# Value products in blocks of four key tiles, and half of half the score tiles copied to SBUF by VectorE

## The chip, the cores and the metric

The kernel runs on one core of one Trainium2 chip. The metric is the device time of one execution in microseconds (us), lower is better. One percent here is 13.8 us.

## The reference

One layer of 2048 rows by 512 columns computes two branches from the same input and blends them row by row with a gate. All tensors are float32.

```python
g = sigmoid((x * gate_w).sum(-1, keepdims=True))
q = (x @ wq).reshape(B, S, H, Dh)      # S 2048, H 32 heads, Dh 16
k, v = x @ wk, x @ wv                  # one key and one value head for all 32
p = softmax(q @ k.T * Dh ** -0.5)      # 32 x 2048 x 2048
a = (p @ v).reshape(B, S, H * Dh) @ wo
b = (silu(x @ w_gate) * (x @ w_up)) @ w_down   # inner width 1792
out = g * a + (1 - g) * b
```

## The kernel before

**The work of the long middle part.** Attention is walked in 512 units: unit `u` is head `u // 16` and key tile `u % 16` of 128 keys. `score(u, j)` makes one score tile: 128 keys by 1024 queries in two banks of PSUM (`pss`), by two TensorE matmuls that use the upper and the lower 64 rows of the array at the same time. ScalarE then takes the exponential of the whole tile from PSUM into the row tile `pt` in SBUF (L613). The pool of `pss` has two buffers, so the matmuls of a score tile wait until the exponential of the tile two before it has read its buffer. `mix(u)` multiplies the exponentials of unit `u` with the values: four matmuls of 32 array columns each, side by side, in full float32, accumulated over the 16 units of a head in `po` (L622). The value tile `vaug` carries columns of ones, so `po` also gets the sums of the softmax.

**The second branch as filler.** The products of the gated feed-forward branch are cut into jobs of 12 or 15 terms (`gate_up`, `down`, and earlier `query`). Each term is split into the upper and the lower 64 rows, and `halves.step` issues one lower half of one job beside one upper half of another: one such step is a *feed*. When a job's last matmul is out, VectorE gets its result from PSUM (`pf`): a copy into `hs` for a gate product (L246), a multiplication for an up product (L257), an addition into `acc` for a down product. The hyperbolic tangent of a gate product runs on ScalarE (L251), and VectorE then forms the SiLU (L252) and splits the product into `hh` and `hl` (L97, L98).

**The order.** It is written by hand under `manual_schedule`: every engine executes its own instructions in the order in which the code issues them. The loop runs over `n` in steps of two units. In each step stand four score tiles, eight feeds, then `mix(u)` and `mix(u + 1)`, which is where the tangents (`ACTS`) and one piece of a finished head's normalization (`LATER`: four reciprocals of 128x128, one product and the store to `o_d`) are issued. Row tiles `pt` have three buffers. The sums of the second branch for all 2048 rows stay in one tile `acc`.

**The tail.** After the loop come the last eight jobs, undivided, and then `finish`, the output projection of the four chunks of rows in the order of `ORDER`.

Of the kernel before, what the change touches and what calls it, by code (L numbers as in the profile page):

```python
# [18 lines left out]
P = 128  # L19
S = 2048  # L20
D = 512
H = 32
# [21 lines left out]
KEEP = 6  # L44
RATE = 8
FIRST = 6
STOP = 5
EARLY = 12
PTB = 3
WRB = 2  # L50


@with_exitstack
def tile_gated_mix(ctx, tc, x, wq, wk, wv, wo, w_gate, w_up, w_down, gate_w, out):
# [35 lines left out]
        return XC[c]  # L90

    wp = tc.alloc_tile_pool(name="wp", bufs=2)
    ACC = []


    def split(hi, lo, src, eng=nc.gpsimd, eng_hi=nc.vector):
# [16 lines left out]
    ACTS, LOADS = [], []  # L113

    def run(queue, n):
        for _ in range(min(n, len(queue))):
            queue.pop(0)()

    def load_split(view, name, bufs, pool=wp):
        shape = list(view.shape)  # L120
# [106 lines left out]

    def open_acc():
        qpool.release()
        accp = tc.alloc_tile_pool(name="accp", bufs=1, side="right")  # L230
        ACC.extend([accp.tile([P, NT, D], F32, name="acc"), accp])

    def gate_up(n, c):
        t = []

        def project(nm):
            def terms():
                r = []
                for k in range(KD):
                    r += three(W[nm, n], XC[c], (slice(None), k), (slice(None), k))  # L240
                return r
            return terms

        def gate(ps):
            g = wp.tile([P, CH], F32, name="hs", bufs=2)
            nc.vector.tensor_copy(g, ps)  # L246

            t.append(wp.tile([P, CH], F32, name="ht", bufs=2))

            def silu():  # L250
                nc.scalar.activation(t[0], g, AF.Tanh, scale=0.5)  # L251
                nc.vector.scalar_tensor_tensor(t[0], t[0], 1.0, g, op0=ALU.add, op1=ALU.mult)  # L252

            ACTS.append(silu)

        def up(ps):
            nc.vector.tensor_tensor(t[0], t[0], ps, ALU.mult)  # L257
            hh = wp.tile([P, CH], F32R, name="hh", bufs=7)
            hl = wp.tile([P, CH], F32R, name="hl", bufs=7)
            split(hh, hl, t[0], nc.vector)  # L260
            HT[n] = (hh, hl)

        r = []
        for nm, end in (("g", gate), ("u", up)):
            r.append(Job(3 * KD, lambda nm=nm: (nm, n) in W and c in XC, project(nm), end))
            r[-1].after.append(lambda nm=nm: load_w(nm, n + 2))
        return r

    def down(ns, c, i):
        t = c * TC + i  # L270

        def ready():
            return all(n in HT and ("d", n) in W for n in ns)

        def terms():
            r = []
            for n in ns:
                r += three(HT[n], W["d", n], (slice(None), slice(i * P, (i + 1) * P)), slice(None))
            return r

        def add(ps):
            acc = ACC[0]
            if ns[0] % NF == 0:
                nc.vector.tensor_scalar(acc[:, t, :], ps, c_sb[:, t:t + 1], None, op0=ALU.mult)
            else:
                nc.vector.scalar_tensor_tensor(acc[:, t, :], ps, c_sb[:, t:t + 1], acc[:, t, :],
                                               op0=ALU.mult, op1=ALU.add)

        return Job(3 * len(ns), ready, terms, add)

    def store_acc(c):
        nc.sync.dma_start(a_d[c], ACC[0][:, c * TC:(c + 1) * TC, :])


    def jobs():
# [23 lines left out]
    def whole(job):  # L319
        for i in range(job.size):  # L320
            job.step(i)
        run(ACTS, 1)


    def fill(n):
# [60 lines left out]
    def finish(c, pool):  # L386
        for i in range(TC):
            t = c * TC + i
            ps = ps_f.tile([P, CH], F32, name="pf")
            terms = []  # L390
            for k in range(KD):
                terms += three([x[:, k] for x in OT[c]], WO[k], (slice(None), slice(i * P, (i + 1) * P)), slice(None))
            mm(ps, terms)
            ot = pool.tile([P, D], F32, name="ot", bufs=4)
            parts = 2 if c == ORDER[-1] and i == TC - 1 else 1
            for j in range(parts):
                w = slice(j * D // parts, (j + 1) * D // parts)
                nc.vector.scalar_tensor_tensor(ot[:, w], ps[:, w], g_sb[:, t:t + 1], ACC[0][:, t, w], op0=ALU.mult, op1=ALU.add)  # L398
                (nc.scalar if j else nc.sync).dma_start(out[t * P:(t + 1) * P, w], ot[:, w])


# [189 lines left out]
    with tc.tile_pool(name="bpool", bufs=2) as bp:  # L591
# [8 lines left out]
                nc.sync.dma_start(qs[b * RT + DH:(b + 1) * RT], qv[b])  # L600


        def score(u, j):
            h, kt = divmod(u, NT)
            if j == 0:
                PT[u] = bp.tile([P, S], F32, name="pt", bufs=PTB)
            ps = ps_s.tile([P, 2 * CH], F32, name="pss")
            for b in range(2):
                rows = slice(b * RT, (b + 1) * RT)
                nc.tensor.matmul(ps[:, b * CH:(b + 1) * CH], ks[rows, kt * P:(kt + 1) * P], QS[h][rows, j, :],  # L610
                                 start=True, stop=True)
            halves.clock += 1
            nc.scalar.activation(PT[u][:, j * 2 * CH:(j + 1) * 2 * CH], ps, AF.Exp, scale=SCALE)  # L613

        def mix(u):
            h, kt = divmod(u, NT)
            pt = PT.pop(u)
            if kt == 0:
                PO[:] = [ps_o.tile([P, CH], F32, name="po")]
            po = PO[0]  # L620
            for c in range(NCH):
                nc.tensor.matmul(po[c * 2 * DH:(c + 1) * 2 * DH, :], vaug[:, kt, :], pt[:, c * CH:(c + 1) * CH],  # L622
                                 start=(kt == 0), stop=(kt == NT - 1))
            if kt == NT - 1:

                osb = hp.tile([P, CH], F32, name="osb")
                nc.vector.tensor_copy(osb, po)
                rsb = hp.tile([P, CH], F32, name="rsb", bufs=1)
                nc.vector.stream_shuffle(rsb, osb, [DH] * 2 * DH)

                def invert(i):
                    w = slice(i * P, (i + 1) * P)
                    nc.vector.reciprocal(rsb[:, w], rsb[:, w])  # L633

                def store():
                    nc.vector.tensor_tensor(osb, osb, rsb, ALU.mult)
# [4 lines left out]
                LATER.extend([lambda i=i: invert(i) for i in range(TC)] + [store])  # L641

        NU = H * NT
        load_head(1)
        for n in range(2):
            load_w("g", n)
# [1 line left out]
        for n in GROUPS[0]:  # L648
            load_w("d", n)
        with tc.manual_schedule():  # L650
            score(0, 0)
            score(0, 1)
            for n in range(NU // 2):
                quota = int((n + 1) * RATE) - int(n * RATE)

                def feed(k):
                    for _ in range(k):
                        if JOBS and n < NU // 2 - STOP or halves.busy():
                            halves.step(n < NU // 2 - STOP)

                u = 2 * n
                if n == 0:
                    feed(FIRST)
                score(u + 1, 0)
                if n == 0:
                    feed(quota - FIRST)
                score(u + 1, 1)
                feed(FIRST)
                if u + 2 < NU:
                    score(u + 2, 0)  # L670
                    feed(quota - FIRST)
                    score(u + 2, 1)
                run(ACTS, len(ACTS))
                mix(u)
                mix(u + 1)
                halves.clock += LONG
                if LATER:
                    LATER.pop(0)()
                if n % (NT // 2) == 1 and 0 < u // NT < H - 1:
                    load_head(u // NT + 1)  # L680
                if n == NU // 2 - EARLY:
                    load_o(ORDER[0], range(KD - 1))
            assert not halves.busy()

    with tc.tile_pool(name="tpool", bufs=2) as tp, tc.manual_schedule():
        for k in range(KD):
            load_wo(k, tp)

        while LATER:
            assert JOBS[0].ready()  # L690
            whole(JOBS.pop(0))
            run(LATER, 1)
        load_o(ORDER[0], [KD - 1])
        while JOBS:
            assert JOBS[0].ready()

            if len(JOBS) == TC:
                load_o(ORDER[1])
            whole(JOBS.pop(0))
        for m, c in enumerate(ORDER):  # L700
            finish(c, tp)
            if m == 1:

# [4 lines left out]
                nc.vector.tensor_scalar(fl[:, 1:2], fl[:, 0:1], LIMIT / SCALE, None, op0=ALU.is_le)  # L708
                nc.vector.tensor_scalar(flag, fl[:, 1:2], -1.0, 1.0, op0=ALU.mult, op1=ALU.add)
            if m + 2 < NCH:  # L710
                load_o(ORDER[m + 2])

    ACC[1].release()
    xpool.release()


# [75 lines left out]
```

## Time and profile before

| | us |
|---|---|
| Median of three executions | 1383.85 |
| The three executions | 1383.24, 1385.38, 1383.85 |
| Span of the profiled execution, first to last instruction | 1379.4 |
| TensorE matmul busy | 1366.2 |
| ScalarE busy | 1019.3 |
| VectorE busy | 524.5 |
| GpSimd busy | 392.0 |

For the profiled execution the page gives the span; a device time of its own is not listed beside it. The median is 4.45 us above the span. Busy TensorE time is counted from a matmul's start to its modelled end, and neighbours overlap, so its 99% says that work is always in flight and not that the array can't be fed faster. Times in timeline rows are starts from the beginning of the span and durations.

### The profile page before, as it was taken

What the parts mean: (1) busy time and instruction counts of PE and PEld (TensorE: products, weight loads), DVE (VectorE), ACT (ScalarE), POOL (GpSimd) and SP (SyncE); (2) the same over time, 40 slices, a digit from 0 to 9 for tenths busy, and PEclk for the clock granted to TensorE, in tenths of its full rate; (3) what the DMA queues carried; (4) which work ended last, traced back from release to release, by engine and by line L of the source; (5) the groups of instructions that cost most, each with busy time, mean ns of one, the idle gap of its engine ahead of it and who ended that gap; (6) DMA issues with size and microseconds to landing.
All of it is one profiled execution on the core that took longest, in us unless ns stands there. A gap on an engine that the chain in (4) does not pass through costs nothing. (4 is left out here: it accounts for less than half of the span.)

```text
span 1379.4 us, 25943 instructions
## 1 busy us (share of the span) xinstructions
PE 1366.2 (99%) x10755; PEld 757.6 (55%) x10755; DVE 524.5 (38%) x868; ACT 1019.3 (74%) x1109; POOL 392.0 (28%) x408
## 2 busy tenths in 40 slices
PE   9999999999999999999999999999999999999998
PEld 7655555555555555555555555555555555555566
DVE  4565333343334333343343253343242343333432
ACT  4577887788787787788787887787787887787500
POOL 6140321241231241241241331241231431332344
PEclk9999999999999999999999999999999999999999
DMA  7456220131141230221241231221221221221144
GB/s 271 146 171 196 75 55 16 51 81 37 46 134 43 73 84 25 58 66 39 66 127 36 74 80 35 54 67 35 66 66 36 89 66 43 50 67 55 42 134 139
DMA packets 101340, 106.69 MB, mean 77 GB/s; under 512 B 9952, under 2 KB 69600, under 8 KB 99680
## 3 DMA queue, kind: packets, MB, share of 16 engines
q1 hardware_dynamic: 99488, 104.76, 26.2%
q8 instruction: 87, 1.43, 0.5%
q10 hardware_dynamic: 1728, 0.20, 0.1%
q14 instruction: 37, 0.30, 0.1%
HBM read 75.04 MB, written 29.36 MB: 76 GB/s over the span
## 5 line engine op out<-in xcount | busy, mean ns | idle before, releaser
L613 ACT ACTIVATE pt<-pss 128x1024 f32<-128x1024 f32 x1024 | 971.7, 1023 | 256.6 <-PE pss L610 248.7
L622 PE MATMUL po<-pt,vaug 128*32 128x512 f32 x4096 | 493.5, 598 | 0.0
L610 PE MATMUL pss<-qs,ks 64*128 64x512 f32 x2048 | 405.8, 431 | 0.4 <-ACT pt L613 0.4
L610 PEld LDWEIGHTS pss<-qs,ks 64*128 64x128 f32 x2048 | 173.4, 184 | 280.1 <-ACT pt L613 260.3
L622 PEld LDWEIGHTS po<-pt,vaug 128*32 128x32 f32 x4096 | 106.9, 109 | 216.1 <-issue 214.4
L161 PE MATMUL pf<-xh,wgl 64*128 64x512 f32 (+1 forms) x444 | 163.3, 390 | 0.4 <-POOL wgl L98 0.4
L161 PE MATMUL pf<-xh,wgh 64*128 64x512 f32 (+1 forms) x444 | 162.7, 389 | 0.0
L161 PE MATMUL pf<-xl,wgh 64*128 64x512 f32 (+1 forms) x444 | 162.3, 390 | 0.0
L161 PE MATMUL pf<-xh,wuh 64*128 64x512 f32 (+1 forms) x440 | 162.2, 389 | 0.0
L161 PE MATMUL pf<-xh,wul 64*128 64x512 f32 (+1 forms) x440 | 161.7, 389 | 0.0
L97 POOL CAST wuh<-wraw 128x512 fp32r<-128x512 f32 x56 | 35.7, 637 | 441.1 <-PE pf L161 330.5
L161 PE MATMUL pf<-wdl,hh 64*128 64x512 f32 (+1 forms) x427 | 157.4, 393 | 2.6 <-POOL wdl L98 2.6
L161 PE MATMUL pf<-xl,wuh 64*128 64x512 f32 (+1 forms) x440 | 159.2, 389 | 0.0
L161 PE MATMUL pf<-wdh,hl 64*128 64x512 f32 (+1 forms) x427 | 156.2, 392 | 0.0
L161 PE MATMUL pf<-wdh,hh 64*128 64x512 f32 (+1 forms) x427 | 155.5, 392 | 0.5 <-POOL wdh L97 0.4
L97 POOL CAST wgh<-wraw 128x512 fp32r<-128x512 f32 x56 | 34.9, 624 | 352.0 <-PE pf L161 244.8
L633 DVE RECIPROCAL rsb<-rsb 128x128 f32<-128x128 f32 x128 | 119.7, 946 | 25.2 <-issue 22.1
L257 DVE TENSOR_TENSOR ht<-ht,pf 128x512 f32<-128x512 f32 x56 | 38.2, 682 | 154.7 <-PE pf L161 154.6
L246 DVE COPY hs<-pf 128x512 f32<-128x512 f32 x56 | 38.4, 685 | 145.5 <-PE pf L161 145.5
L161 PEld LDWEIGHTS pf<-xh,wgl 64*128 64x128 f32 (+1 forms) x444 | 81.8, 184 | 10.6 <-POOL wgl L98 0.8
L161 PEld LDWEIGHTS pf<-xl,wgh 64*128 64x128 f32 (+1 forms) x444 | 81.9, 184 | 9.7
L161 PEld LDWEIGHTS pf<-xh,wgh 64*128 64x128 f32 (+1 forms) x444 | 81.8, 184 | 9.8 <-POOL wgh L97 0.2
(151 smaller groups left out, 1535.8 us busy)
## 6 DMA issues: line engine op xcount, KB each, us to landing
wraw<-in_B_w_gate_dram SPq DMA_DIRECT2D x56, 256.0 KB
wraw<-in_B_w_up_dram SPq DMA_DIRECT2D x56, 256.0 KB
wraw<-in_B_w_down_dram SPq DMA_DIRECT2D x56, 256.0 KB
qs<-q_d SPq DMA_DIRECT2D x62, 192.0 KB
q_d<-hl SPq DMA_DIRECT2D x18, 256.0 KB
q_d<-hh SPq DMA_DIRECT2D x18, 256.0 KB
o_d<-osb SPq DMA_DIRECT2D x128, 32.0 KB
a_d<-acc SPq DMA_DIRECT2D x4, 1024.0 KB
```

What stands on the lines that cost most here:

```text
L97: eng_hi.tensor_copy(hi, src)
L161: ins = nc.tensor.matmul(self.ps, a, b, start=(i == 0 and not half), stop=(last and half != 0))
L246: nc.vector.tensor_copy(g, ps)
L257: nc.vector.tensor_tensor(t[0], t[0], ps, ALU.mult)
L610: nc.tensor.matmul(ps[:, b * CH:(b + 1) * CH], ks[rows, kt * P:(kt + 1) * P], QS[h][rows, j, :], start=True, stop=True)
L613: nc.scalar.activation(PT[u][:, j * 2 * CH:(j + 1) * 2 * CH], ps, AF.Exp, scale=SCALE)
L622: nc.tensor.matmul(po[c * 2 * DH:(c + 1) * 2 * DH, :], vaug[:, kt, :], pt[:, c * CH:(c + 1) * CH], start=(kt == 0), stop=(kt == NT - 1))
L633: nc.vector.reciprocal(rsb[:, w], rsb[:, w])
```

## The change

**Blocks.** For the first 32 units the loop is as before. From unit 32 on, `block(k, ...)` handles four units: it issues eight score tiles and 16 feeds in the order of the string `STEPS` (S is a score tile, F a feed), and then four `mix` in a row. The score tiles run two units ahead of the products, as before. The first block takes ten score tiles (`TURN`) and the last takes four. To hold six row tiles, `pt` alternates between two pools of three buffers.

**Halves.** `KINDS` names the eight score tiles of a block: for an H tile (0, 1, 2, 4 and 5) VectorE copies the second 512 columns out of PSUM into `pt` (L656), ScalarE takes the exponential of the first 512 columns from PSUM, and later the exponential of the copied 512 columns in place in SBUF. An A tile (3, 6 and 7) is taken whole, as before. `EXPS` is ScalarE's order: `4d` is what is read from PSUM of tile 4, `4s` is the half in SBUF.

**VectorE's other work.** The SiLU, the split into `hh` and `hl` and the pieces of `LATER` go into queues with a cost each, and up to `BUDGET` of them are issued at the end of a block, ahead of the four `mix` in program order. The copy of `po` out of PSUM moves to just after the second score tile of the next block.

**Room.** The sums of the second branch are held in three buffers of one chunk each in place of one tile. The first chunk is stored to `a_d`, as before, and read back in the tail; `finish` takes the chunks in the order of `OUTS`.

```diff
-STOP = 5
-EARLY = 12
+BLOCK = 4
+BEGIN = 16
+STOP = 2
+EARLY = 6
+OUTS = (1, 2, 3, 0)
+STEPS = "SSFFFFSFFSFFSFFFSFFFSFFS"
+KINDS = "HHHAHHAA"
+EXPS = ("0d", "1d", "0s", "2d", "3d", "4d", "1s", "5d", "6d", "7d", "2s", "4s", "5s")
+TURN = "SS" + "SFF" * 8
+BUDGET = 3.6
...
-            def silu():
-                nc.scalar.activation(t[0], g, AF.Tanh, scale=0.5)
-                nc.vector.scalar_tensor_tensor(t[0], t[0], 1.0, g, op0=ALU.add, op1=ALU.mult)
-            ACTS.append(silu)
+            def tanh():
+                if len(t) == 2:
+                    nc.scalar.activation(t[0], g, AF.Tanh, scale=0.5)
+                    DEFER.append((0.7, silu))
...
+            def cast():
+                split(hh, hl, t[0], nc.vector)
+                HT[n] = (hh, hl)
+            DEFER.append((1.6, cast))
...
-        def score(u, j):
+        def score(u, j, half=False):
...
-            nc.scalar.activation(PT[u][:, j * 2 * CH:(j + 1) * 2 * CH], ps, AF.Exp, scale=SCALE)
+            pt = PT[u][:, j * 2 * CH:(j + 1) * 2 * CH]
+            if half:
+                nc.vector.tensor_copy(pt[:, CH:], ps[:, CH:])
+            return pt, ps
+
+        def exps(pt, ps, w=slice(None)):
+            nc.scalar.activation(pt[:, w], ps[:, w], AF.Exp, scale=SCALE)
...
+        def block(k, first, last, steps, kinds, order):
...
+            for i, what in enumerate(steps):
+                if what == "F":
+                    feed(1, more)
+                elif len(made) < len(tiles):
+                    made.append(score(*tiles[len(made)], kinds[len(made)] == "H"))
+                    emit()
+                if len(made) > 1:
+                    run(COPY, 1)
...
+            run(ACTS, len(ACTS))
...
+            left = BUDGET
+            for queue in (LATER[:1], DEFER, LATER):
+                while queue and queue[0][0] <= left:
+                    cost, f = queue.pop(0)
+                    left -= cost
+                    f()
...
+            for u in range(BLOCK * k, BLOCK * (k + 1)):
+                mix(u)
...
-            for n in range(NU // 2):
+            for n in range(BEGIN):
...
+            for k in range(2 * BEGIN // BLOCK, NB):
+                u = BLOCK * k
+                if k == 2 * BEGIN // BLOCK:
+                    n = u + 6 - (u + 1)
+                    block(k, u + 1, u + 6, TURN, "A" * 2 * n, [f"{i}d" for i in range(2 * n)])
+                elif k == NB - 1:
+                    block(k, u + 2, u + 4, STEPS, "AAAA", ("0d", "1d", "2d", "3d"))
+                else:
+                    block(k, u + 2, u + 6, STEPS, KINDS, EXPS)
```

`emit` issues the entries of `EXPS` in their order, each as soon as its tile has been issued. Two places show what the change makes of the engines' own orders. The name behind "waits" is the engine whose signal an instruction waits for.

ScalarE in the middle of the loop, before: whole tiles of 1024 columns out of PSUM, each released by TensorE, and a tangent between them.

```order
L613 ACTIVATE pt<-pss 128x1024 [waits PE_49]
L251 ACTIVATE ht<-hs 128x512 [waits DVE_49]
L613 ACTIVATE pt<-pss 128x1024 [waits PE_49,Activation_49]
L613 ACTIVATE pt<-pss 128x1024 [waits PE_49]
L613 ACTIVATE pt<-pss 128x1024 [waits PE_49,Activation_49]
L613 ACTIVATE pt<-pss 128x1024 [waits PE_49]
```

ScalarE now, from the last four score tiles of one block (5d, 6d, 7d and the three halves 2s, 4s, 5s, then a tangent) into the next (0d, 1d, 0s, 2d, 3d, 4d, 1s):

```order
L660 ACTIVATE pt<-pss 128x512 [waits DVE_49]
L660 ACTIVATE pt<-pss 128x1024 [waits PE_49,Activation_49]
L660 ACTIVATE pt<-pss 128x1024 [waits PE_49]
L660 ACTIVATE pt<-pt 128x512 x3
L268 ACTIVATE ht<-hs 128x512
L660 ACTIVATE pt<-pss 128x512 [waits DVE_49,Activation_49]
L660 ACTIVATE pt<-pss 128x512 [waits DVE_49]
L660 ACTIVATE pt<-pt 128x512
L660 ACTIVATE pt<-pss 128x512 [waits DVE_49]
L660 ACTIVATE pt<-pss 128x1024 [waits PE_49]
L660 ACTIVATE pt<-pss 128x512 [waits DVE_49]
L660 ACTIVATE pt<-pt 128x512
```

Three of the eight tiles of a block are still released by TensorE; the first halves of the other five are released by VectorE. Counted through the built program, the signal that such a half waits for is that of VectorE's copy of the second half of the same tile.

VectorE in the middle of the loop, before: the reciprocals of `LATER`, the results of the feed jobs, and the SiLU behind its tangent (the row that waits for ScalarE).

```order
L357 MEMSET sign 1x1 [waits PE_49]
L633 RECIPROCAL rsb<-rsb 128x128
L246 COPY hs<-pf 128x512 [waits PE_49]
L357 MEMSET sign 1x1 [waits DVE_49,PE_49]
L252 SCALAR_TENSOR_TENSOR ht<-ht,hs 128x512 [waits Activation_49]
L633 RECIPROCAL rsb<-rsb 128x128
L257 TENSOR_TENSOR ht<-ht,pf 128x512 [waits DVE_49,PE_49]
```

VectorE now, over the end of one block and the first score tiles of the next:

```order
L394 MEMSET sign 1x1 [waits DVE_49,PE_49]
L688 STREAM_SHUFFLE rsb<-osb 128x512 [waits DVE_49]
L276 SCALAR_TENSOR_TENSOR ht<-ht,hs 128x512 [waits DVE_49,Activation_49]
L679 RECIPROCAL rsb<-rsb 128x128 [waits DVE_49]
L679 RECIPROCAL rsb<-rsb 128x128
L656 COPY pt<-pss 128x512 [waits PE_49] x2
L323 SCALAR_TENSOR_TENSOR acc<-pf,c_sb,acc 128x512 [waits PE_49]
L656 COPY pt<-pss 128x512 [waits PE_49]
L394 MEMSET sign 1x1 [waits PE_49]
L656 COPY pt<-pss 128x512 [waits PE_49] x2
```

The copies of score tiles (L656) stand in the same row of instructions as the rest of VectorE's work, and the first two copies of a block stand behind what the block before has deferred, here a SiLU that waits for the tangent and two reciprocals.

More of the change, by code (lines that the diff above doesn't have):

```diff
@@ L117, in run, with settle @@
             queue.pop(0)()
+    def settle():
+        run(ACTS, len(ACTS))
+        while DEFER:
+            DEFER.pop(0)[1]()
     def load_split(view, name, bufs, pool=wp):
@@ L229, in open_acc @@
         qpool.release()
-        accp = tc.alloc_tile_pool(name="accp", bufs=1, side="right")
-        ACC.extend([accp.tile([P, NT, D], F32, name="acc"), accp])
+        for name in ("accp", "bp2"):
+            PAIR.append(tc.alloc_tile_pool(name=name, bufs=3, side="right"))
     def gate_up(n, c):
@@ L281, in add @@
         def add(ps):
-            acc = ACC[0]
+            if c not in ACC:
+                ACC[c] = PAIR[0].tile([P, TC, D], F32, name="acc")
+            acc = ACC[c]
             if ns[0] % NF == 0:
-                nc.vector.tensor_scalar(acc[:, t, :], ps, c_sb[:, t:t + 1], None, op0=ALU.mult)
+                nc.vector.tensor_scalar(acc[:, i, :], ps, c_sb[:, t:t + 1], None, op0=ALU.mult)
             else:
-                nc.vector.scalar_tensor_tensor(acc[:, t, :], ps, c_sb[:, t:t + 1], acc[:, t, :],
+                nc.vector.scalar_tensor_tensor(acc[:, i, :], ps, c_sb[:, t:t + 1], acc[:, i, :],
                                                op0=ALU.mult, op1=ALU.add)
@@ L321, in whole @@
             job.step(i)
-        run(ACTS, 1)
+        settle()
     def fill(n):
@@ L394, in finish @@
             ot = pool.tile([P, D], F32, name="ot", bufs=4)
-            parts = 2 if c == ORDER[-1] and i == TC - 1 else 1
+            parts = 2 if c == OUTS[-1] and i == TC - 1 else 1
             for j in range(parts):
                 w = slice(j * D // parts, (j + 1) * D // parts)
-                nc.vector.scalar_tensor_tensor(ot[:, w], ps[:, w], g_sb[:, t:t + 1], ACC[0][:, t, w], op0=ALU.mult, op1=ALU.add)
+                nc.vector.scalar_tensor_tensor(ot[:, w], ps[:, w], g_sb[:, t:t + 1], ACC[c][:, i, w], op0=ALU.mult, op1=ALU.add)
                 (nc.scalar if j else nc.sync).dma_start(out[t * P:(t + 1) * P, w], ot[:, w])
@@ L600, in load_head, with new_pt @@
                 nc.sync.dma_start(qs[b * RT + DH:(b + 1) * RT], qv[b])
-        def score(u, j):
+        def new_pt(u):
+            late = u > PTB * (BEGIN * 2 // PTB) and (u - 2 * BEGIN) % (2 * PTB) >= PTB
+            PT[u] = (PAIR[1] if late else bp).tile([P, S], F32, name="pt", bufs=PTB)
+        def score(u, j, half=False):
             h, kt = divmod(u, NT)
             if j == 0:
-                PT[u] = bp.tile([P, S], F32, name="pt", bufs=PTB)
+                new_pt(u)
             ps = ps_s.tile([P, 2 * CH], F32, name="pss")
@@ L639, in store, with feed @@
                                           osb[c * 2 * DH:c * 2 * DH + DH, :])
-                LATER.extend([lambda i=i: invert(i) for i in range(TC)] + [store])
+                COPY.append(lambda: nc.vector.tensor_copy(osb, po))
+                LATER.extend([(0.6, lambda: nc.vector.stream_shuffle(rsb, osb, [DH] * 2 * DH))] +
+                             [(1.0, lambda i=i: invert(i)) for i in range(TC)] + [(0.7, store)])
         NU = H * NT
+        NB = NU // BLOCK
+        COPY = []
+        def feed(k, more=True):
+            for _ in range(k):
+                if JOBS and more or halves.busy():
+                    halves.step(more)
@@ new lines, in block, with emit @@
+        def block(k, first, last, steps, kinds, order):
+            more = k < NB - STOP
+            tiles = [(u, j) for u in range(first, last) for j in range(2)]
+            order = list(order)
+            made = []
+            def emit():
+                while order and int(order[0][0]) < len(made):
+                    i, how = int(order[0][0]), order.pop(0)[1]
+                    pt, ps = made[i]
+                    if how == "s":
+                        exps(pt, pt, slice(CH, None))
+                    else:
+                        exps(pt, ps, slice(0, CH) if kinds[i] == "H" else slice(None))
+            for i, what in enumerate(steps):
[5 more added lines that the diff above has]
+                if len(made) > 1:
+                    run(COPY, 1)
+            due = [e for e in order if int(e[0]) < 2 * (BLOCK * (k + 1) - first)]
+            for e in due:
+                order.remove(e)
+            rest, order[:] = order[:], due
+            emit()
+            run(ACTS, len(ACTS))
+            order[:] = rest
+            emit()
+            assert not order and len(made) == len(tiles)
+            left = BUDGET
[4 more added lines that the diff above has]
+                    f()
+                if queue is not DEFER and queue is not LATER and left < BUDGET:
+                    LATER.pop(0)
+            for u in range(BLOCK * k, BLOCK * (k + 1)):
+                mix(u)
+            halves.clock += 2 * LONG
@@ L650, in tile_gated_mix @@
         with tc.manual_schedule():
-            score(0, 0)
-            score(0, 1)
-            for n in range(NU // 2):
[L654 to L659, printed above, removed]
+            for j in range(2):
+                exps(*score(0, j))
+            for n in range(BEGIN):
+                quota = RATE
                 u = 2 * n
@@ L663, in tile_gated_mix @@
                     feed(FIRST)
-                score(u + 1, 0)
+                exps(*score(u + 1, 0))
                 if n == 0:
                     feed(quota - FIRST)
-                score(u + 1, 1)
+                exps(*score(u + 1, 1))
                 feed(FIRST)
[L669 to L673, printed above, removed]
+                exps(*score(u + 2, 0))
+                feed(quota - FIRST)
+                exps(*score(u + 2, 1))
+                settle()
                 mix(u)
@@ L676, in tile_gated_mix @@
                 halves.clock += LONG
+                run(COPY, 1)
                 if LATER:
[L678 to L682, printed above, removed]
-            assert not halves.busy()
-    with tc.tile_pool(name="tpool", bufs=2) as tp, tc.manual_schedule():
+                    LATER.pop(0)[1]()
+                if n == NT // 2 + 1:
+                    load_head(2)
+            assert PAIR
+            for k in range(2 * BEGIN // BLOCK, NB):
[5 more added lines that the diff above has]
+                    block(k, u + 2, u + 4, STEPS, "AAAA", ("0d", "1d", "2d", "3d"))
+                else:
+                    block(k, u + 2, u + 6, STEPS, KINDS, EXPS)
+                h = u // NT
+                if k % (NT // BLOCK) == 0 and 0 < h < H - 1:
+                    load_head(h + 1)
+                if k == NB - EARLY:
+                    load_o(OUTS[0], range(KD - 1))
+            assert not halves.busy()
+            run(COPY, 1)
+            settle()
+            print("steps", halves.steps, "idle", halves.idle, "left", len(JOBS))
+    PAIR.pop().release()
+    with tc.tile_pool(name="tpool", bufs=2) as tp, tc.tile_pool(name="rpool", bufs=1, side="right") as rp, \
+            tc.manual_schedule():
         for k in range(KD):
             load_wo(k, tp)
+        ACC[0] = rp.tile([P, TC, D], F32, name="again")
         while LATER:
@@ L691, in tile_gated_mix @@
             whole(JOBS.pop(0))
-            run(LATER, 1)
-        load_o(ORDER[0], [KD - 1])
+            LATER.pop(0)[1]()
+            if LATER:
+                LATER.pop(0)[1]()
+        load_o(OUTS[0], [KD - 1])
         while JOBS:
@@ L697, in tile_gated_mix @@
             if len(JOBS) == TC:
-                load_o(ORDER[1])
+                load_o(OUTS[1])
             whole(JOBS.pop(0))
-        for m, c in enumerate(ORDER):
+        nc.sync.dma_start(ACC[0], a_d[0])
+        for m, c in enumerate(OUTS):
             finish(c, tp)
```

30 lines of the change are left out of this document (20 added, 10 removed).

## The prediction

> **What bounds the kernel now.** I read the page's shares and groups first, then TensorE's timeline over two steps of the loop, then ScalarE's.
>
> ```profile
> span 1379.4 us, 25943 instructions
> ...
> PE 1366.2 (99%) x10755; PEld 757.6 (55%) x10755; DVE 524.5 (38%) x868; ACT 1019.3 (74%) x1109; POOL 392.0 (28%) x408
> ...
> L613 ACT ACTIVATE pt<-pss 128x1024 f32<-128x1024 f32 x1024 | 971.7, 1023 | 256.6 <-PE pss L610 248.7
> ```
>
> ScalarE's exponentials wait for score tiles (248.7 us); TensorE is what is late. One step of two units, from TensorE's timeline (matmuls, and two rows of weight loads):
>
> ```profile
> 504.49 0.74 PE L610 MATMUL pss<-qs,ks 64*128 64x512 f32 x4
> 505.06 0.39 PE L161 MATMUL pf<-xh,wul 64*128 64x512 f32 x1
> 505.30 0.39 PE L161 MATMUL pf<-xh,wuh 64*128 64x512 f32 x1
> ...
> 506.45 0.40 PE L610 MATMUL pss<-qs,ks 64*128 64x512 f32 x2
> ...
> 507.14 0.44 PE L610 MATMUL pss<-qs,ks 64*128 64x512 f32 x2
> 507.51 1.92 PE L622 MATMUL po<-pt,vaug 128*32 128x512 f32 x16
> 509.37 0.74 PE L610 MATMUL pss<-qs,ks 64*128 64x512 f32 x4
> ```
> ```profile
> 503.09 0.13 PEld L622 LDWEIGHTS po<-pt,vaug 128*32 128x32 f32 x4 [0.30 <-issue]
> 503.52 0.13 PEld L622 LDWEIGHTS po<-pt,vaug 128*32 128x32 f32 x4 [0.30 <-issue]
> ```
>
> A step takes 509.37 - 504.49 = 4.88 us. Feeds and score pairs follow each other at 0.231 us (505.06 to 506.45 is six of them), and a product group of four at 0.43. Twelve slots and four groups would be 12 x 0.231 + 4 x 0.43 = 4.49. The other 0.39 is paid once for each visit to the products: the last pair to the first product takes 0.37, the products 1.86 in place of 1.72, and the first two pairs with what follows them 0.57 in place of 0.46. No buffer is late: ScalarE has finished before the products end.
>
> ```profile
> 505.09 3.79 ACT L613 ACTIVATE pt<-pss 128x1024 f32<-128x1024 f32 x4 [1.10 <-PE pss L610]
> 509.97 1.95 ACT L613 ACTIVATE pt<-pss 128x1024 f32<-128x1024 f32 x2 [1.08 <-PE pss L610]
> ```
>
> So one exponential takes 1.02 (the group's mean), the next follows it at (3.79 - 1.02) / 3 = 0.92, 1.08 us of each step is idle, and the first starts 0.60 after its pair.
>
> **Part 1: fewer visits.** 120 blocks take the place of 240 steps. Each saves one visit, 0.39: -47 us if TensorE keeps its pace, from 9.76 to 9.37 a block.
>
> **Part 2: the score tiles' turnaround.** This term decides. The row orders show that the first half of an H tile waits for VectorE's copy of its second half, so copy and exponential stand one behind the other, and the buffer goes back only after both. With two buffers each pair waits for the tile two before it. The prices:
>
> ```profile
> L246 DVE COPY hs<-pf 128x512 f32<-128x512 f32 x56 | 38.4, 685 | 145.5 <-PE pf L161 145.5
> L251 ACT ACTIVATE ht<-hs 128x512 f32<-128x512 f32 x56 | 35.4, 632 | 11.1 <-DVE hs L246 11.1
> ...
> 39.80 0.60 ACT L197 ACTIVATE hh<-pf 128x512 fp32r<-128x512 f32 x1 [1.54 <-PE pf L161]
> 40.29 0.68 ACT L198 ACTIVATE hl<-pf,kmax 128x512 fp32r<-128x512 f32 x1
> ...
> 502.01 0.39 PE L161 MATMUL pf<-xh,wul 64*128 64x512 f32 x1
> 502.23 0.47 PE L610 MATMUL pss<-qs,ks 64*128 64x512 f32 x2
> 502.44 0.69 DVE L257 TENSOR_TENSOR ht<-ht,pf 128x512 f32<-128x512 f32 x1 [1.46 <-PE pf L161]
> 513.65 0.63 ACT L251 ACTIVATE ht<-hs 128x512 f32<-128x512 f32 x1
> 514.31 0.69 DVE L252 SCALAR_TENSOR_TENSOR ht<-ht,hs 128x512 f32<-128x512 f32 x1 [2.02 <-ACT ht L251]
> ```
>
> The copy is the form of L246: 0.69. No half exponential is in the trace; 512 columns out of PSUM take 0.60 (L197), out of SBUF 0.63 (L251), and the next may start 0.49 after the first. I take 0.60 and 0.63, pitch 0.49 and 0.52. VectorE starts 0.04 after a matmul's end (502.01 + 0.39 to 502.44) and 0.03 after ScalarE's (513.65 + 0.63 to 514.31); I take 0.04 for each hand-over and 0.05 towards TensorE. A pair that had waited takes 0.47.
>
> By hand through a plain block, from the start of its first pair at 0: copy 0 runs 0.55 to 1.24, exponential 0d 1.28 to 1.88, so the third pair, whose slot is at 1.50, starts at 1.93. Copy 1 ends at 1.93, 1d at 2.57, 0s at 3.09. Copy 2 runs 2.44 to 3.13 and 2d ends at 3.77; the fourth pair is on time at 2.62, the fifth, due at 3.31, starts at 3.82. 3d ends at 4.68, and the sixth pair is on time at 4.74. Copy 4 ends at 5.02, 4d at 5.66; the seventh starts at 5.71, 0.05 late. 1s then 5d end at 6.67; the eighth, due at 6.40, starts at 6.72. The products start at 7.09, and their eight groups and the way back take 1.86 + 4 x 0.43 = 3.58: the next block starts at 10.66. ScalarE's rest (6d, 7d, 2s, 4s, 5s) ends at 10.07, under the products. ScalarE's price for five tiles in two pieces, 5 x (0.49 + 0.52 - 0.92) = 0.45, lies there too. 10.66 - 9.76 = +0.90 a block, times 120: **+108 us**, the 47 saved included. Three turnarounds of 1.89 to 1.93 stand where the slots leave 4.73 us for three; at 1.71 each the gain would just be eaten. With the cheapest row at every place (0.39, 0.69, 0.60 and 0.03 a hand-over) one is 1.77 and the block still loses 0.3, +36.
>
> **Part 3: what stands ahead of the copies on VectorE.** In a block with a tangent, ScalarE reaches it after 5s: it ends at 10.59, and the SiLU, which waits for it on VectorE, at 11.31 (0.69). The next block's copy 0 would have started at 10.66 + 0.55 = 11.21. What follows the SiLU before that copy is added in full, since the third pair waits for it:
>
> ```profile
> L633 DVE RECIPROCAL rsb<-rsb 128x128 f32<-128x128 f32 x128 | 119.7, 946 | 25.2 <-issue 22.1 <-DVE acc L286 1.6
> L97 DVE CAST hh<-ht 128x512 fp32r<-128x512 f32 x56 | 58.4, 1043 | 1.9
> L98 DVE TENSOR_TENSOR hl<-ht,hh 128x512 fp32r<-128x512 f32 x56 | 48.1, 859 | 1.9
> L636 DVE TENSOR_TENSOR osb<-osb,rsb 128x512 f32<-128x512 f32 x32 | 25.3, 789 | 13.7 <-issue 12.4 <-DVE acc L286 0.8
> ```
>
> In the changed program's row order the 56 SiLU have behind them: nothing more 24 times (0.10 late each), two reciprocals 12 times (2.0), the cast and subtraction 8 times (2.0), one reciprocal 6 times (1.05), a reciprocal and the product 3 times (1.8), the product 3 times (0.9). Sum **+57 us**. If the tangent ran early it would be nothing.
>
> The feeds' results are taken in line between the copies: 1.33 a block (16 feeds over 12). From the three feeds after the fifth pair one (0.69) pushes copy 5 by 0.4 at the eighth pair, from the first four it pushes copy 2 by 0.1; elsewhere it falls into gaps. 1.33 x (3/16 x 0.4 + 4/16 x 0.1) = 0.13 a block: **+15 us**, with bounds of 0 and, every one in full, 1.33 x 0.69 x 120 = 110.
>
> **Part 4: the rest.** The first block's ten whole tiles keep ScalarE 9.2 us, and its products wait: +2. GpSimd and the weight loads keep their counts and have longer blocks. The first chunk's sums are read back behind the last job on SyncE's queue, with three chunks of output projection to cover them; ahead of them stand loads that the tail had before. Uncovered, a megabyte at the tail's rate is 7 us:
>
> ```profile
> 1340.00:1379.00 39.00, 33.06 (x144) 26.12 (x142) 9.74 (x17) 0.00 (x0) 15.08 (x16) 0.96 0.46 144
> ```
>
> I take 0, and the same for a cheaper tail. The stores of a finished head move within SyncE's queue by a block at most, and only the tail reads them. The copy of `po` moves behind copy 1, four and a half us ahead of the products that need the buffer; in 31 blocks it pushes copy 2 by some 0.1 us, 3 us in all, which I leave out.
>
> **The sum.** 108 + 57 + 15 + 2 = +182 on the profiled span of 1379.4: 1561. With the 4.45 by which the median stands above that span: **1566 us**.
>
> **The clock.** In the tail before, a stretch of 3.41 us with TensorE busy for 1.81 was followed by half clock for 6.83; one busy for 2.06 was not.
>
> ```profile
> 1311.35:1314.76 3.41, 1.81 (x5) 0.67 (x4) 3.34 (x5) 0.00 (x0) 3.11 (x4) 1.00 0.38 102
> 1314.76:1321.59 6.83, 5.41 (x12) 3.62 (x13) 2.12 (x2) 0.00 (x0) 3.01 (x4) 0.50 0.41 122
> ...
> 7.46:10.87 3.41, 2.06 (x18) 1.66 (x18) 3.27 (x10) 1.58 (x2) 0.00 (x0) 1.00 0.98 321
> ```
>
> In the 23 blocks in which copy 0 is late by 1.8 us or more, the third pair starts at 3.8 in place of 1.93, while the last feed ahead of it has started at 1.26 and ended at 1.65: TensorE is idle for 2.1 us, more than the 1.60 of that stretch. A stretch of 3.41 us that contains all of it comes about (3.41 - 2.1) / 3.41 = 4 times in 10, so some 9 times, and half clock for 3.41 to 6.83 us of work that also waits for copies costs 1.7 to 3.4 each: 0 to 31 us. I take 0 in the sum and keep 31 for the range. The Trainium skill's "TensorE: Matmul & The Clock Gate" (Why this matters for your kernels) allows idle gaps up to about 3 us before the clock falls; by it this term is nothing. The trace differs: none of the gaps in that stretch reached 1.2 us.
>
> **Rivals.** *Copy and exponential side by side: faster.* If VectorE's copy were done by the time ScalarE comes to its tile, as when ScalarE runs a tile behind, the third pair would be on time from a turnaround of 1.58 us down, and each block would take 9.37: 1383.85 - 47 + 2 = 1339. ScalarE's sum allows it: 3 x 0.92 + 5 x (0.49 + 0.52) = 7.8 and a tangent. Against it: after the products ScalarE is idle and no tile is in hand, and the program makes 0d wait for copy 0. The Trainium skill's "PSUM — Partial Sum Buffer" (Specifications) says that both engines read PSUM in parallel at full bandwidth when their banks differ, as these halves' do; no run here shows it. 0.09.
>
> *The tangents don't hold up the copies.* VectorE gets through its queue in the products' 3.6 us; part 2 alone: 1383.85 + 108 + 2 = 1494. For it: half of the SiLU have nothing behind them. 0.08.
>
> *Turnarounds near 1.71 us:* gain and stall cancel, 1384, with 1375 to 1480 between. It needs copy and exponential each 0.1 below their rows. 0.04, half of it slower, half the same.
>
> *The clock falls often,* at twice the 31 us or more, or the in-line results push a copy half of the time: 1615 to 1650. For it: idle gaps of 2.1 us that the loop did not have. Against it: in a plain block no wait is longer than 0.5 us. 0.07.
>
> **How the numbers follow.** The forecast, the turnaround with the queue on VectorE, has 0.72. The range, 1480 to 1612, takes in the cheap turnaround (36 + 57 + 2) and the second rival below, and above the clock's 31 with 15 more for in-line results of twice the price; it leaves out the first, third and fourth, 0.20. About 0.2%, 2.8 us, is what a measurement can tell from no change: faster 0.09, same 0.02, slower 0.89.
>
> **What would show it.** Right: TensorE's score pairs (L651) wait for ScalarE, a plain block takes 10.5 to 10.8 us, blocks that follow a tangent up to 12.6, VectorE's copies take 0.69, and ScalarE's half tiles wait for VectorE. Wrong: half exponentials that start with their copies, blocks of 9.4 us, or copies that never stand behind a SiLU.

## The result and the profile after

The changed kernel takes 1565.38 us (median of four executions, 1565.26 to 1565.71); the kernel before, run beside it, takes 1383.55. The ratio is 1.1316, with a 95% interval from 1.13 to 1.1332. The profiled execution spans 1563.7 us, 184.3 more than before.

From the page of the kernel after, its span, its shares and the groups that answer to those of before (busy time, mean ns of one, idle time ahead and what ended it):

```profile
span 1563.7 us, 26910 instructions
...
PE 1433.5 (92%) x10755; PEld 761.6 (49%) x10755; DVE 862.9 (55%) x1458; ACT 1089.2 (70%) x1699; POOL 389.0 (25%) x408
...
L660 ACT ACTIVATE pt<-pss 128x512 f32<-128x512 f32 (+1 forms) x1024 | 746.1, 779 | 371.6 <-DVE pt L656 337.5
L656 DVE COPY pt<-pss 128x512 f32<-128x512 f32 x590 | 395.3, 687 | 363.1 <-PE pss L651 356.5
L651 PE MATMUL pss<-qs,ks 64*128 64x512 f32 x2048 | 454.9, 457 | 117.6 <-ACT pt L660 113.4
...
L660 ACT ACTIVATE pt<-pt 128x512 f32<-128x512 f32 x590 | 345.8, 637 | 0.0
```

TensorE falls from 99% to 92% of a longer span. The ring of waits is in three rows: TensorE's score matmuls wait 113.4 us for ScalarE's exponentials (0.4 before), ScalarE waits 337.5 us for VectorE's copies, and the copies wait for TensorE. No engine is full; each waits for the next. GpSimd, the feeds and the products keep their counts. The score matmuls' row of before, for comparison:

```profile
L610 PE MATMUL pss<-qs,ks 64*128 64x512 f32 x2048 | 405.8, 431 | 0.4 <-ACT pt L613 0.4
```

Two rows from the longer list of groups are VectorE's split, the work that can stand behind a SiLU:

```profile
L106 DVE TENSOR_TENSOR hl<-ht,hh 128x512 fp32r<-128x512 f32 x56 | 42.4, 758 | 1.9
L105 DVE CAST hh<-ht 128x512 fp32r<-128x512 f32 x56 | 34.2, 611 | 1.3 <-DVE pt L656 0.5 <-DVE ht L286 0.3
```

A plain block, one that nothing from the block before delays, from the timeline of the kernel after (start, duration, engine, line, operation, count, idle time ahead and its releaser; feeds and weight loads left out):

```profile
866.68 0.73 PE L651 MATMUL pss<-qs,ks 64*128 64x512 f32 x4
867.29 1.29 DVE L656 COPY pt<-pss 128x512 f32<-128x512 f32 x2 [1.27 <-PE pss L651]
868.02 1.19 ACT L660 ACTIVATE pt<-pss 128x512 f32<-128x512 f32 x2 [2.02 <-DVE pt L656]
868.67 0.50 PE L651 MATMUL pss<-qs,ks 64*128 64x512 f32 x2 [0.34 <-ACT pt L660]
869.11 0.62 ACT L660 ACTIVATE pt<-pt 128x512 f32<-128x512 f32 x1
869.21 0.69 DVE L656 COPY pt<-pss 128x512 f32<-128x512 f32 x1 [0.63 <-PE pss L651]
...
870.58 0.50 PE L651 MATMUL pss<-qs,ks 64*128 64x512 f32 x2 [0.27 <-ACT pt L660]
...
872.57 0.50 PE L651 MATMUL pss<-qs,ks 64*128 64x512 f32 x2
873.57 0.50 PE L651 MATMUL pss<-qs,ks 64*128 64x512 f32 x2
874.01 3.64 PE L670 MATMUL po<-pt,vaug 128*32 128x512 f32 x32
...
877.58 0.73 PE L651 MATMUL pss<-qs,ks 64*128 64x512 f32 x4
```

The block takes 877.58 - 866.68 = 10.90 us, against 9.76 for two steps before. Copy 0 begins at 867.29, its exponential only at 868.02, behind the copy, and the third pair at 868.67, 1.99 after the first. The fifth starts at 3.90 and the seventh at 5.89: three turnarounds of 1.99, 1.91 and 1.99.

A block behind a tangent, with two reciprocals deferred with the SiLU, from the same timeline:

```profile
1002.46 0.69 DVE L276 SCALAR_TENSOR_TENSOR ht<-ht,hs 128x512 f32<-128x512 f32 x1 [3.31 <-ACT ht L268]
1002.58 0.73 PE L651 MATMUL pss<-qs,ks 64*128 64x512 f32 x4
...
1003.07 1.75 DVE L679 RECIPROCAL rsb<-rsb 128x128 f32<-128x128 f32 x2
...
1004.75 1.22 DVE L656 COPY pt<-pss 128x512 f32<-128x512 f32 x2
1005.47 1.13 ACT L660 ACTIVATE pt<-pss 128x512 f32<-128x512 f32 x2 [3.04 <-DVE pt L656]
...
1006.12 0.50 PE L651 MATMUL pss<-qs,ks 64*128 64x512 f32 x2 [1.89 <-ACT pt L660]
...
1015.96 0.51 PE L651 MATMUL pss<-qs,ks 64*128 64x512 f32 x2
```

Copy 0 starts 2.17 after the block's first pair, in place of 0.61, and TensorE stands for 1.89 us. This block takes 13.38. Part of that is the clock, as the windows of the same execution show (length, TensorE busy and its matmuls, granted clock, DMA share, GB/s):

```profile
457.94:461.35 3.41, 1.51 (x14) 1.00 0.00 0
707.11:710.52 3.41, 1.55 (x14) 1.00 0.09 19
1004.07:1007.48 3.41, 1.52 (x14) 1.00 0.00 0
1007.48:1010.89 3.41, 3.31 (x18) 0.50 0.00 0
365.78:369.19 3.41, 1.88 (x14) 1.00 0.00 0
369.19:372.60 3.41, 3.36 (x28) 1.00 0.03 7
```

A stretch of 3.41 us with 1.52 busy was followed by one at half clock; one with 1.88 was not. The loop has eight such spells.

### The profile page after: what moved, and what is told of

It is laid out like the page before. It is cut to its first block, busy times and chain, and to the rows that moved or that the text cites. A ratio compares the mean times of both kernels' runs of the same rounds, so it can differ in the third digit from the quotient of the medians.

```text
span 1563.7 us, 26910 instructions
## 1 busy us (share of the span) xinstructions
PE 1433.5 (92%) x10755; PEld 761.6 (49%) x10755; DVE 862.9 (55%) x1458; ACT 1089.2 (70%) x1699; POOL 389.0 (25%) x408
## 5 line engine op out<-in xcount | busy, mean ns | idle before, releaser
L660 ACT ACTIVATE pt<-pss 128x512 f32<-128x512 f32 (+1 forms) x1024 | 746.1, 779 | 371.6 <-DVE pt L656 337.5
L656 DVE COPY pt<-pss 128x512 f32<-128x512 f32 x590 | 395.3, 687 | 363.1 <-PE pss L651 356.5
L651 PE MATMUL pss<-qs,ks 64*128 64x512 f32 x2048 | 454.9, 457 | 117.6 <-ACT pt L660 113.4
L670 PE MATMUL po<-pt,vaug 128*32 128x512 f32 x4096 | 467.7, 596 | 0.0
L651 PEld LDWEIGHTS pss<-qs,ks 64*128 64x128 f32 x2048 | 185.5, 186 | 442.1 <-ACT pt L660 329.4
L660 ACT ACTIVATE pt<-pt 128x512 f32<-128x512 f32 x590 | 345.8, 637 | 0.0
L670 PEld LDWEIGHTS po<-pt,vaug 128*32 128x32 f32 x4096 | 119.5, 110 | 258.1 <-issue 257.8
L276 DVE SCALAR_TENSOR_TENSOR ht<-ht,hs 128x512 f32<-128x512 f32 x48 | 34.1, 711 | 133.2 <-ACT ht L268 133.2
L174 PEld LDWEIGHTS pf<-xl,wuh 64*128 64x128 f32 (+1 forms) x440 | 83.4, 190 | 7.7
L174 PEld LDWEIGHTS pf<-xh,wuh 64*128 64x128 f32 (+1 forms) x440 | 83.5, 190 | 7.0
```

The source lines that it names most:

```text
L174: ins = nc.tensor.matmul(self.ps, a, b, start=(i == 0 and not half), stop=(last and half != 0))
L656: nc.vector.tensor_copy(pt[:, CH:], ps[:, CH:])
L660: nc.scalar.activation(pt[:, w], ps[:, w], AF.Exp, scale=SCALE)
```

## The experiments

My theory was the prediction's: (a) the first half's exponential stands behind VectorE's copy, and this chain makes the turnarounds; (b) VectorE's queue makes some copies late. The rivals were that blocks of four themselves lose the time, or that VectorE and ScalarE slow each other where they read score tiles at the same time. Each edit is against the changed kernel unless another is named.

**Halves in buffers of their own.** Each score tile becomes two tiles of one bank, so that the first half waits for TensorE alone. A whole tile then takes two exponentials.

```diff
-            ps = ps_s.tile([P, 2 * CH], F32, name="pss")
+            ps = [ps_s.tile([P, CH], F32, name=f"pss{'xy'[b]}") for b in range(2)]
...
-                nc.vector.tensor_copy(pt[:, CH:], ps[:, CH:])
+                nc.vector.tensor_copy(pt[:, CH:], ps[1])
```

> The changed kernel with each half of a score tile in a PSUM tile of its own (one bank), so that the exponential of a first half no longer waits for VectorE's copy of the second half; whole tiles are taken in two exponentials of 512 columns. Theory (the buffer's turnaround, copy and exponential one behind the other): the third pair is on time at 1.5 us, plain blocks take 9.3 to 9.6 us, and only copies that stand late behind a SiLU still cost, some 40 to 50 us in all: 1375 to 1400 us. Rival A (ScalarE's extra instructions are the bound): it has the same work and somewhat more, so nothing changes, 1565 or above. Rival B (VectorE's load makes every copy late): 1500 or above.

It took 1399.51 us, ratio 1.0121 (1.0104 to 1.0137): 166 us less than the change. Its blocks have a median of 9.68 and a minimum of 9.33. Its groups on the page:

```profile
L664 ACT ACTIVATE pt<-pssx 128x512 f32<-128x512 f32 x1024 | 595.5, 603 | 165.6 <-PE pssy L653 115.9 <-PE pssx L653 35.6 <-issue 8.4
L658 DVE COPY pt<-pssy 128x512 f32<-128x512 f32 x590 | 392.6, 685 | 241.6 <-PE pssy L653 178.2
```

ScalarE's exponentials out of PSUM are now released by TensorE and no longer by the copy, and the copy still takes 685 ns and the exponential 603 while the two run side by side: 505 of the 590 copies overlap an exponential out of PSUM by more than 0.3 us, and none of these takes more than 694 ns. So the engines don't slow each other here, and most of the lost time is the chain. The Trainium skill's "PSUM — Partial Sum Buffer" (Specifications) says that they read in parallel when the banks differ; these two rows agree. What made the changed kernel wait was the program's dependency by tile, not the memory. The edit also lets each matmul of a pair wait for its own half's buffer alone, which no run separates; an estimate from the rows of the changed kernel says that a plain block doesn't need it, since a copy and an exponential that start together at 0.61 are over at 1.3, before the third pair's slot at 1.5.

**Control: whole tiles in two pieces, and nothing else.**

```diff
-            nc.scalar.activation(pt[:, w], ps[:, w], AF.Exp, scale=SCALE)
+            for b in range(2) if w == slice(None) else [w.start // CH]:
+                c = slice(b * CH, (b + 1) * CH)
+                nc.scalar.activation(pt[:, c], ps[b] if isinstance(ps, list) else ps[:, c], AF.Exp, scale=SCALE)
```

> The changed kernel with only its whole tiles taken in two exponentials of 512 columns, the control of the kernel with split PSUM tiles. All theories: three more instructions of ScalarE a block, 0.07 us each on its queue, 1565 to 1590 us.

One execution took 1573.62 us. The two pieces, which the experiment above needs as well, gain nothing by themselves.

**Blocks of four alone, every score tile whole.**

```diff
-KINDS = "HHHAHHAA"
-EXPS = ("0d", "1d", "0s", "2d", "3d", "4d", "1s", "5d", "6d", "7d", "2s", "4s", "5s")
+KINDS = "AAAAAAAA"
+EXPS = ("0d", "1d", "2d", "3d", "4d", "5d", "6d", "7d")
```

> The changed kernel with every score tile whole: no copies, no halves, still blocks of four. Theory: a whole tile's turnaround is 1.6 us, so TensorE runs ahead until ScalarE's queue of eight tiles at 0.92 sets the last pair: it starts at 6.3 and the next block at 10.2, since ScalarE has only two tiles left under the products: 1430 to 1455 us. Rival A (the extra instructions of ScalarE are the bound): ScalarE's work falls to 7.4 a block, TensorE is the bound again at 9.4, about 1340.

It took 1441.11 us, ratio 1.0422 (1.0404 to 1.0439). From its timeline, one block:

```profile
664.39 0.74 PE L651 MATMUL pss<-qs,ks 64*128 64x512 f32 x4
...
665.00 7.44 ACT L660 ACTIVATE pt<-pss 128x1024 f32<-128x1024 f32 x8 [2.33 <-PE pss L651]
...
670.65 0.50 PE L651 MATMUL pss<-qs,ks 64*128 64x512 f32 x2
671.09 3.64 PE L670 MATMUL po<-pt,vaug 128*32 128x512 f32 x32
...
674.65 0.73 PE L651 MATMUL pss<-qs,ks 64*128 64x512 f32 x4
```

ScalarE takes its eight tiles in one run, 0.92 apart, then has nothing for 2.33 us. The eighth pair needs six of them done: 0.61 + 6 x 0.92 + 0.1 = 6.2 after the block's start (670.65 - 664.39 = 6.26), and products and way back bring it to 10.26. So with two score buffers a block of four by itself costs 59 us (1441.11 against 1382.36 beside it): under eight products ScalarE has only two tiles to work on. Halves were meant to take that load off ScalarE; chained behind copies, they cost another 124, the late copies of the next experiment among them.

**The tangent earlier,** ahead of the last three halves, so that the SiLU is over before the next block's copies.

```diff
                 while order and int(order[0][0]) < len(made):
+                    if order[0] == "2s":
+                        run(ACTS, len(ACTS))
```

> The changed kernel with the tangent issued ahead of ScalarE's last three halves (2s, 4s, 5s) in place of behind them, so that the SiLU can run under the products and nothing waits for it at the block's end. Theory: the tangent ends 1.5 us earlier, so copies behind a cast are on time and those behind two reciprocals late by 0.2 us; plain blocks stay at 10.9: 38 us of late copies and 8 us of half clock go but for some 3, 1518 to 1528. Rival A (ScalarE's work is the bound): 1565. Rival B (VectorE's load makes the copies late wherever the SiLU stands): 1550 or above.

It took 1521.95 us, ratio 1.1 (1.0981 to 1.1018): 43 less than the change. Blocks have a mean of 10.97, none of 119 is above 11.8 but the first, and no half-clock spell is left in the loop. Late copies with the clock that they cause are worth 43 us.

**The SiLU after the deferred work,** a block later.

```diff
             emit()
-            run(ACTS, len(ACTS))
...
+            run(ACTS, len(ACTS))
             for u in range(BLOCK * k, BLOCK * (k + 1)):
```

> The changed kernel with the tangents issued behind the deferred VectorE work, so that a SiLU is deferred to the next block and no copy stands behind one that waits. Theory: plain blocks stay at 10.9, the blocks of 11.3 to 13.7 us go, with them the spells of half clock: 38 + 8 us less, 1512 to 1527. Rival A (ScalarE's work): unchanged, 1560 to 1570. Rival B (copies late behind VectorE's queue are the main cost): 1420 or less.

It took 1533.92 us, ratio 1.1089 (1.107 to 1.1107), 7 above the expected range. From its timeline:

```profile
660.23 0.74 PE L651 MATMUL pss<-qs,ks 64*128 64x512 f32 x4
...
662.42 1.29 POOL L106 TENSOR_TENSOR wul<-wraw,wuh 128x512 fp32r<-128x512 f32 x1
...
662.65 1.61 DVE L276 SCALAR_TENSOR_TENSOR ht<-ht,hs 128x512 f32<-128x512 f32 x1
...
664.97 0.69 DVE L656 COPY pt<-pss 128x512 f32<-128x512 f32 x1
...
666.34 0.50 PE L651 MATMUL pss<-qs,ks 64*128 64x512 f32 x2 [2.46 <-ACT pt L660]
...
674.45 0.74 PE L651 MATMUL pss<-qs,ks 64*128 64x512 f32 x4
```

The SiLU now sometimes stands in line ahead of copy 2, here with 1.61 us in place of 0.69, and this block takes 14.22, the longest of the run. TensorE stands for 2.46 us in it, and the granted clock is 0.50 for 3.41 us from 667.41 on, the only such spell in this run's loop. Waiting was only moved to another place in the queue.

**Twice the copies,** each copy issued a second time.

```diff
                 nc.vector.tensor_copy(pt[:, CH:], ps[:, CH:])
+                nc.vector.tensor_copy(pt[:, CH:], ps[:, CH:])
```

> The changed kernel with every copy of a half score tile issued twice, the second writing the same data again. Theory: copy and exponential stand in series in each turnaround, so three turnarounds a block grow by 0.65 to 0.7 each: blocks of 12.9, 1780 to 1830 us. If only VectorE's total load mattered (it is busy for 55% of the span, and five more copies add 3.4 us to a block of 10.9), the time would stay below 1600.

One execution took 1930.62 us. Its rows in the list of waits (total, count, longest):

```profile
ACT pt L661 <- DVE pt L657: 611.2, 479, 4.9
PE pss L651 <- ACT pt L661: 389.4, 541, 2.6
```

The added copies lengthen the wait of ScalarE and then that of TensorE, as copies off the path would not. Its shortest full blocks take 13.53, 2.6 above the change's and 0.6 above the estimate; the mean is 14.40, since more copies are late, and 27 spells of half clock fall into its loop. I had the direction and underrated the size; no run shows where the further 0.6 comes from.

**Both mended:** the first experiment's buffers by bank, with the tangent early in its `emit`.

```diff
                 while order and int(order[0][0]) < len(made):
+                    if order[0] == "2s":
+                        run(ACTS, len(ACTS))
```

> Both: each half of a score tile in a PSUM tile of its own, and the tangent ahead of the last three halves. Theory: TensorE is the bound again, plain blocks at 9.37, with some in-line VectorE results left: 9.4 to 9.6 on the mean, 1343 to 1362 us, faster than before the change by 1.5 to 3%. Rival A and B: no faster than with the split tiles alone, 1395 to 1400.

It took 1363.85 us, ratio 0.986 (0.9844 to 0.9877): faster than both kernels, and 2 us above the range. A plain block from its timeline:

```profile
526.54 0.49 PE L653 MATMUL pssx<-qs,ks 64*128 64x512 f32 x1
...
527.11 2.08 DVE L658 COPY pt<-pssy 128x512 f32<-128x512 f32 x3
...
527.13 1.08 ACT L664 ACTIVATE pt<-pssx 128x512 f32<-128x512 f32 x2 [0.83 <-PE pssy L653]
...
528.03 0.39 PE L653 MATMUL pssx<-qs,ks 64*128 64x512 f32 x1
...
535.95 0.50 PE L653 MATMUL pssx<-qs,ks 64*128 64x512 f32 x1
```

Exponential and copy start 0.02 apart, the third pair comes 1.49 after the first, which is its slot, and the block takes 9.41. In its timeline about four blocks of ten lose some 0.35 us where a pair's second matmul waits for a copy that stands behind a feed's result on VectorE.

**One feed moved** in that version, from just ahead of the last score pair to just ahead of the fifth.

```diff
-STEPS = "SSFFFFSFFSFFSFFFSFFFSFFS"
+STEPS = "SSFFFFSFFSFFFSFFFSFFFSFS"
```

> The kernel with split PSUM tiles and the early tangent, and one feed moved from ahead of the last score pair to ahead of the fifth. There, in 4 of 10 blocks, the pair's second matmul waits 0.35 us or more for VectorE's copy of tile 2, which stands behind a feed's result. Theory (only these in-line results keep the blocks from 9.37): most of the 0.27 us a block above 9.37 goes, 1340 to 1355 us. If the blocks above 9.4 come from elsewhere: 1360 to 1367.

It took 1361.58 us, ratio 0.9847 (0.9834 to 0.986). The interval overlaps that of the version before it, so no gain is shown. The median block fell from 9.65 to 9.55 and the mean only from 9.64 to 9.61: the waits at the fifth pair are mostly gone, but 35 of the 59 blocks that had taken about 9.38 now take 9.5 or more, 9.59 in the middle. What the rest of the way to 9.37 costs stays open.

## Why the prediction was right

**The bound and part 1** hold. The saving of 0.39 a visit is real: with the waits removed (both mended), plain blocks take 9.37 to 9.39, where 9.37 was worked out. In the changed kernel nothing of it is left.

**Part 2, the turnaround,** is the mechanism, shown by the first experiment; the term was too small. A plain block takes 10.89, not 10.66, so it is 1.13 a block and some +135 us where the sum had +108. Copies and exponentials have their prices (687 and 637 ns). What was off are small things: the first exponential starts at 1.33 to 1.34, not 1.28, in most plain blocks because it follows copy 0 by 0.09 and not 0.04, in the block shown and a few others because copy 0 starts at 0.61 and not 0.55; pairs that had waited take 0.50, not 0.47; turnarounds are 1.91 to 1.99, not 1.89 to 1.93; the products start 0.44 behind the last pair, not 0.37. So a plain block also lies 0.1 above the 10.5 to 10.8 that had been set as the sign of being right.

Two side sums of the prediction don't follow from its own walk, in which the eighth pair waits for exponential 5d, 1.01 behind 4d. With that wait the block of the cheapest rows (a turnaround of 1.77) takes 10.27, so it loses 0.5 and not 0.3, and the turnaround at which the gain is eaten is about 1.60, not 1.71. The forecast uses neither.

**Part 3, late copies,** is right in kind and too large. By block lengths above 10.89: 12 with two reciprocals 1.48 each (clock apart) for 2.0; 8 with cast and subtraction 1.12 for 2.0, because these two take 0.61 and 0.76 on average in the rows above and not the 1.04 and 0.86 of before; 6 with one reciprocal 0.67 for 1.05; 3 with the product 0.46 for 0.9; 3 with both 1.51 (clock apart) for 1.8; the rest 0.03. The sum is 37, where 57 stood. The in-line results cost 0.11 in 65 blocks without a SiLU, some 7 for 15.

**The clock** was taken as 0 in the sum, though some 9 spells were worked out; eight came. With two reciprocals a block with a spell takes 13.3 to 13.4, one 13.75, where its like without takes 12.37, so a spell costs about 1.0 us, below the 1.7 to 3.4 that I had set, and all of them 8. By the Trainium skill's "TensorE: Matmul & The Clock Gate" (Why this matters for your kernels), with its gaps of up to about 3 us, none would have come; here TensorE stood for 1.89 us and the clock fell.

**The sum.** The first block is 2.8 longer than a step pair and was given 2. 135 + 37 + 7 + 8 + 3 = 190, against 182 predicted; the loop's last product starts at 1483.7 in place of 1298.1, 185.6 later, and the span is 184.3 longer. Of the 4 to 6 us between, some 3 are the last block: it takes four whole tiles and is 1.9 shorter than the two steps that it replaces, where the sum has it 1.13 longer. The rest I leave unassigned. That the forecast lies 0.6 us from the median is luck: a turnaround term 27 too low met queue terms 28 too high and a clock of 8 left out. The mechanism was right; the terms were less exact than that distance suggests.

**The rivals.** Side by side did not happen in the change, for the reason given, the wait on the copy; the mended version shows that it happens when the program allows it. The tangents do hold up copies (43 us less with the early tangent). Turnarounds near 1.71 and an often lower clock are excluded by the rows above.

## What to carry to other kernels

Splitting a tile between two engines shortened its turnaround here only once both halves were released by the producer: give each engine a tile of its own, and look at whose signal each half waits for. Before grouping work to save visits, walk one group through its buffers and ask how much the neighbour still has in hand while the long visit lasts. In an engine's queue that runs in order, what waits for another engine belongs where nothing urgent stands behind it: the place of the tangents was worth 43 us here, and 36 with the split tiles.

## What the hardware showed beside this

**The clock fell after less than 2 us of idle time.** The eight stretches of 3.41 us ahead of the loop's half-clock spells have TensorE busy for 1.51 to 1.56, each with one gap of 1.85 to 1.90; the next least, 1.88 busy, was not followed by a spell. With the copies doubled the line is not as sharp: 1.60 was not followed and 1.92 was. So no threshold is shown.

**VectorE's SiLU stretches beside GpSimd.** In the run with the SiLU a block later, the SiLU of 1.61 us overlaps a subtraction on GpSimd (L106, 662.42). Over that run, 26 of the 48 SiLU of this line (L276) have no such neighbour and take at most 0.69; 22 with one take 0.70 to 1.76, while 145 copies out of PSUM (L656) beside the same GpSimd operation take at most 0.69. The Trainium skill's "GPSIMD Engine Reference" (1. Specifications) says that the two contend for SBUF where VectorE reads two SBUF inputs, which the SiLU does and the copy doesn't; the counts agree. This adds up to some 15 us of longer SiLU in that run, and I take it as the likely reason for the 7 us missed there, which no run separates.
